# An attention and two expert layers on one core: low halves of w1's block sums on VectorE, and a new order

## The chip, the cores and the metric

The kernel runs on one NeuronCore of one Trainium2 chip. The metric is the device time of one execution in microseconds (us); lower is better. The engines are TensorE (PE; its weight loads are PEld), VectorE (DVE), ScalarE (ACT), GpSimd (POOL) and SyncE (SP), each with a queue of its own that it works through in order. DMAs are issued from SP's and POOL's queues; 16 DMA engines carry them.

## What is computed

Attention first: 2 batches, 8 heads, 768 positions, head size 64. Each query sees the keys less than 16 positions away and 24 block summaries (keys by maximum, values by mean over blocks of 32). Its result, 1536 rows of 512, passes through two layers of experts:

```python
# layer 1: E = 4 experts, D = 512, F = 1024
p = domain_probs / (domain_probs.sum(-1, keepdims=True) + 1e-09)
for e in range(E):
    h = np.maximum(x @ w1[e], 0.0)
    out += p[:, e:e + 1] * (h @ w2[e])
# layer 2: the same with 8 experts; P comes from softmax-like logits
# x @ w_gate and 8 rounds of row and column normalization
```

All inputs and the output are float32.

## The kernel before

**Products.** Rows are taken in two blocks of 768 (b = 0, 1). The hidden size is cut into units of 256 columns: 4 experts x 4 units in layer 1, 8 x 4 in layer 2, 48 units. A step is one unit with one block, so there are 96 steps. In each step a 2x2 block product is made by a scheme of seven products with sums of blocks in place of eight. The seven operands on the side of the weights are the blocks A11, A12, A22 and the sums S1, S2, S3, S4. Each product runs in three parts, because a float32 operand is split into a high half (rounded to the format float32r) and a low half (what is left): high x high, high x low, low x high. `product` (L294 is its matmul) makes the first product, x with w1: seven calls of six matmuls. `add_second` (L593) makes the product with w2: seven operands, two column halves, three matmuls each. One step is 84 matmuls of 128x384. Between them `add_hop` takes the rectified and weighted results (the quads q11 to q22), forms their seven block sums on DVE, and splits each into halves: the high one by ACT (`hi_op`, L453), the low one by DVE (`lo_op`, L443 and L448).

**Weights.** `add_weights(u, kind, start)` (L455) brings the weights of unit u, kind 1 for w1 and 2 for w2. SP loads four blocks into one of three raw buffers (two named `raw`, the third is `xf` once the attention is done with it). The inner function `group` splits n blocks: ACT copies them as the high half (L471), ACT writes their negative into the place of the low half, rounded in the same way (L472), and POOL issues a DMA that adds the raw blocks onto it (L475). What stays is the rest of the rounding. First this is done for the three plain blocks; then three adding DMAs in the raw buffer (L482) turn the raw blocks into sums; then `group` is called for the pair S1, S2 (slots 6 and 7 of `wop`) and the pair S4, S3 (slots 8 and 9). The plain blocks have two sets of slots, by turns; the sums have one, so that a pair can be written only when PE has finished with the last unit's pair.

**The order.** Nothing is issued as the code is read. `op`, `vop` (DVE) and `aop` (ACT) enter each operation into a list with its engine, a name in the table `SPAN`, what it reads and writes, and a due time in units of a step. `run_work` (L367) then plans: it always takes the operation that can start earliest by the prices of `SPAN`, and of several with the same start the one with the earliest due time, and issues it. So the prices and due times alone fix the order in every queue. An entry of `SPAN` is (busy time, time until the result is there). DMAs have four numbers: busy, time until the transfer starts, the length of the transfer on one shared line of DMAs, and the time to landing after that. `add1` to `add3` are the adding DMAs, with lengths of ADD, 2 ADD and 3 ADD.

**Constants.** `ALONG` is the span of due times of the attention, in steps, `XDUE`, `W0DUE` and `FIRST0` the due times of the first operands, weights and products beside it. `NARROW` is the pair of heads from which the attention has five banks of PSUM and not eight. `XPOOL` names the low halves of x that POOL makes. `FIRST` is the order of the seven first products. `HOP`, `GOFF`, `DCOFF`, `LEAD` and `LEAD2` are offsets of the hop, the second products, their second column half, the weights' loads, and the weights' sums. `LATER` and `SOONER` shift the steps around `border`, the last step of layer 1. There `add_turn` makes the next layer's x, and `add_gate` and `add_sinkhorn` its shares.

Of the kernel before, what the change touches and what calls it, by code (L numbers as in the profile page):

```python
# [9 lines left out]
F32 = mybir.dt.float32  # L10
# [8 lines left out]
def local_global_attention_moe_moe(  # L19
# [86 lines left out]
    def wkey(kind, u, a):  # L106
        s = slot(u, a)
        return ("w", kind, s // 3 if s < 6 else 2 + (s - 6) // 2)
# [24 lines left out]
    for b in range(2):  # L133
        for j, name in enumerate(("c22", "c12", "z", "m2", "m1")):
            for c in range(KH):
                i = j * KH + c
# [131 lines left out]
    def pair_of(kind, u, i):  # L268
        r = raw_of(kind, u)
        return ((r[:, 1:3], (1, 2)), (r[:, 0:4:3], (0, 3)))[i]  # L270
# [36 lines left out]
    def relu(S, out, src, th, neg=False):  # L307
# [9 lines left out]

    ADD = 0.72  # L320
    SPAN = {
# [5 lines left out]
        "v1536": (1.3, 1.34), "vmax": (0.57, 0.65), "vsum": (0.57, 0.66), "vrec": (0.12, 0.18),  # L327
        "vks": (0.6, 0.69), "vks2": (0.35, 0.42), "vkw": (0.7, 0.81), "vq": (1.0, 1.1),
        "vvb": (0.22, 0.3), "vmk": (0.82, 0.83), "vid": (1.1, 1.15),
        "a": (0.41, 0.48), "ah": (0.42, 0.52), "a512": (0.53, 0.63), "a768": (0.74, 0.84),  # L330
        "as": (0.2, 0.26), "akw": (0.8, 0.91), "aq": (0.95, 1.04), "aexp": (1.05, 1.12),
        "ax": (0.31, 0.38),
        "p256": (0.75, 0.77), "p384": (1.05, 1.08), "psm": (0.98, 1.02), "pks": (0.8, 0.85),
        "pid": (0.55, 0.6), "p1": (0.2, 0.25), "pmask": (3.0, 3.1), "psel": (0.9, 0.95),
        "add1": (0.87, 1.2, ADD, 1.2), "add2": (0.87, 1.2, 2 * ADD, 1.2),
        "add3": (0.87, 1.2, 3 * ADD, 1.2), "ld": (0.45, 1.0, 0.6, 1.8), "st": (0.45, 0.5, 0.5, 1.2),
        "ldk": (0.45, 1.0, 0.8, 1.2), "ldv": (0.45, 1.0, 1.3, 1.2), "lds": (1.4, 1.6, 1.2, 1.2),
        "ldp": (0.45, 1.0, 0.5, 1.2),
    }
    HOP_WAIT = 0.09  # L340
    work = []
# [94 lines left out]
    def aop(fn, reads, writes, due, span="a", use=None):  # L436
        op("ACT", span, reads, writes, due, fn, use=use)
# [17 lines left out]
    def add_weights(u, kind, start):  # L455
        hi, lo = wop[kind]
        i = turn_of(kind, u)
        R = [("raw", i, j) for j in range(4)]
        for o, x, blocks in loads(kind, u):
            first = XF if (kind, u) == (1, 2) else []  # L460
            op(
                "SP", "ld", [("mark", WAIT0)] if u == 0 else (),
                [R[j] for j in blocks] + first, start,
                lambda o=o, x=x: nc.sync.dma_start(out=o, in_=x),
            )

        def group(s, src, blocks, key, due, span):
            n = len(blocks)
            h, l = hi[:, s:s + n], lo[:, s:s + n]
            rd = [R[j] for j in blocks]  # L470
            aop(lambda: nc.scalar.copy(out=h, in_=src), rd, [key + ("hi",)], due, span)  # L471
            aop(lambda: nc.scalar.mul(l, src, -1.0), rd, [key + ("lo",)], due, span)  # L472
            op(
                "POOL", f"add{n}", rd, [key + ("lo",)], due + 0.05,
                lambda: nc.gpsimd.dma_start(out=l, in_=src, accum_op=ALU.add),  # L475
            )

        group(slot(u, A12), raws[i][:, 0:3], (0, 1, 2), wkey(kind, u, A12), start + 0.2, "a768")
        for o, x, wr, rd in sums_of(kind, u):
            op(  # L480
                "POOL", f"add{len(wr)}", [R[j] for j in (*rd, *wr)], [R[j] for j in wr], start + 0.5,
                lambda o=o, x=x: nc.gpsimd.dma_start(out=o, in_=x, accum_op=ALU.add),  # L482
            )
        group(6, *pair_of(kind, u, 0), wkey(kind, u, S1), start + LEAD2, "a512")
        group(8, *pair_of(kind, u, 1), wkey(kind, u, S4), start + LEAD2 + 0.1, "a512")

    def wk(kind, u, x):
        k = wkey(kind, u, x)
# [506 lines left out]
    def add_loads(i, d):  # L995
        b, hp = pairs[i]
        for j in range(2):
            op(
                "SP", "ldk", (), [("kn", j)] + ([("mark", i)] if j else []), d,
                lambda j=j: nc.sync.dma_start(  # L1000
                    out=kn[:, :, j, :], in_=k[b, 2 * hp + j].rearrange("(c p) d -> p c d", p=P)
                ),
            )
        for j in range(2):
            op(
                "SP", "ldk", (), [("qn", j)], d + 0.01,
                lambda j=j: nc.sync.dma_start(
                    out=qn[:, j],
                    in_=q[b, 2 * hp + j].rearrange("(c p r) d -> p c (r d)", p=P, r=2),
                ),  # L1010
            )
        op(
            "SP", "ldv", (), ["vn"], d + 0.3,
            lambda: nc.sync.dma_start(
                out=vn, in_=v[b, 2 * hp:2 * hp + 2].rearrange("h (p c) d -> p h c d", c=VC)
            ),
        )
        t = vs[i % 2]

        def windows(j):  # L1020
            src = v[b, 2 * hp + j]
            mid = bass.AP(
                src.tensor, src.offset + (QT - WIN) * D, [[D, KW], [QT * D, NQ - 2], [1, D]]
            )
            nc.sync.dma_start(out=t[0:KW, 0, j, :], in_=src[0:KW, :])
            nc.sync.dma_start(out=t[0:KW, 1:NQ - 1, j, :], in_=mid)
            nc.sync.dma_start(out=t[0:KW, NQ - 1, j, :], in_=src[S - KW:S, :])

        for j in range(2):
            op("SP", "lds", (), [("vs", i % 2, j)], d + 0.35, lambda j=j: windows(j))  # L1030

    def add_keys(i, d):
# [50 lines left out]
        def spread():  # L1083
# [4 lines left out]
                )  # L1088

        op(  # L1090
            "POOL" if KSPOOL else "DVE", "pks" if KSPOOL else "vks",
            [("ks", p, 0), ("ks", p, 1)], [("kw", p, 2)], d + 0.03, spread,
        )

# [152 lines left out]
    def add_rows_first(d):  # L1247
# [15 lines left out]
                in1=dsum[:, :, None].to_broadcast([P, NTT, E1]), op=ALU.mult,  # L1263
            )

        vop(shares, ["dp"], ["p1"], d, "v768", True)
        tk = take_of(0)
        n = E1 * NTT
        op(
# [22 lines left out]
            )  # L1292

        aop(halves, ["wg"], ["wghi"], d + 4.0, "as")
        vop(lows, ["wghi", "ident"], ["wghl"], d + 4.0, "vs", True)

    def set_places():

# [18 lines left out]
    L = E1 * NFU - 1  # L1317
    steps = [(u, b, 2 * u + b) for u in range(NU) for b in range(2)]
    border = 2 * L + 1
    FIRST = {0: "1567324", 1: "1562374"}  # L1320
    SECOND = {0: "1256437", 1: "1524637"}
    HOP, GOFF, DCOFF, LEAD, LEAD2 = 1.15, 0.16, 3.9, 1.0, 0.97
    LOPOOL = ()
    ALONG = 8.8
    NARROW = 4
    WAIT0 = 2
    KSPOOL = False
    XDUE = [-5.4, -2.8, -2.0, 0.3]
    W0DUE = -3.0
    FIRST0 = -1.1  # L1330
    XPOOL = [(B22, T3), (N1, B21, T3, N4), (T3, N4), (B22, N4)]
    LATER = {1: -0.4, 2: -0.4, 3: 0.6, 8: -0.4}
    SOONER = {0: 0.4, 2: -0.4, 3: -0.4, 6: 0.2, 7: 0.2}
    TURN = 0.8
    M2ACT = True
    with tc.manual_schedule():
        ps = ctx.enter_context(tc.tile_pool(name="ps", bufs=1, space=PSUM))
        full = [ps.tile([P, 512], F32, name=f"bank{i}") for i in range(8)]
# [33 lines left out]
        op("SP", "ld", ["prow1"], [("pb", 1)], -0.5, lambda: load_row(PB[1], 0, 0, 1))  # L1372
        for j, key in enumerate(("pz", ("bank", 3), ("bank", 4), ("bank", 5), ("bank", 6))):
            op(
                "PE", "one", [("x", 0, 0, B11)] + wk(1, 0, A11), [key], 0.1,
                lambda j=j: nc.tensor.matmul(
                    cut[2 + j], wop[1][0][:, SLOT[A11], 0:P], x_of(0, 0, 0, B11),
                    start=True, stop=True, skip_group_check=True,
                ),
            )  # L1380
# [65 lines left out]
```

## Time and profile before

| | |
|---|---|
| median of 3 runs | 1564.73 us (1563.39 to 1567.13) |
| profiled execution | 1563.7 us, span 1562.0 us |
| PE, PEld busy | 1522.5, 1489.1 us |
| DVE, ACT, POOL busy | 1303.5, 1201.3, 608.7 us |
| DMA | 231.13 MB, mean 148 GB/s |
| granted clock of PE, mean | 0.997 |

Busy time is the union of an engine's instructions within the span; issuing instructions of a queue's sequencer are not counted. The ends of matmuls are modelled, so the idle time of PE is what can be read, not how near it is to its peak. A wait names the instruction or DMA that ended it. Names of tiles are the program's own, without numbers: `w2lo` is the low half of w2's operands, `bank` a bank of PSUM, `hoph` a half of a hop operand, `vn` the tile of v.

### The profile page before, as it was taken

The numbers are of one execution on the slowest core, as the hardware profiler recorded it, in microseconds if no ns is written. First come the engines' busy times: TensorE is split into PE (matmuls) and PEld (weight loads), VectorE is DVE, ScalarE is ACT, GpSimd is POOL, SyncE is SP. The second block draws the span as 40 slices with busy tenths as digits, with TensorE's granted clock in tenths as the row PEclk, the third lists the DMA queues.
The fourth block names the chain that finished last, engine by engine and source line by source line (L and its number), as shares of the span: only waits on it lengthen the run. The fifth ranks groups of instructions, "written<-read, shape, count | busy, mean of one in ns | idle before, by whom it ended". The sixth has DMA issues, their size and how long they took to land.

```text
span 1562.0 us, 26666 instructions
## 1 busy us (share of the span) xinstructions
PE 1522.5 (97%) x9106; PEld 1489.1 (95%) x9106; DVE 1303.5 (83%) x2717; ACT 1201.3 (77%) x2587; POOL 608.7 (39%) x632
## 2 busy tenths in 40 slices
PE   8899999999999999999999999999999999999998
PEld 7799999999999988999999999999999999999997
DVE  7787788788888897899888888888888887888888
ACT  6798688687777779777777778777877877868865
POOL 3553434434343332333343343443434343443430
PEclk9999999999999999999999999999999999999999
DMA  9978888878778874697878778878878887888863
GB/s 213 219 152 148 149 154 149 150 146 153 147 149 149 149 130 94 120 182 133 149 142 156 149 139 161 153 139 155 146 139 159 149 145 150 150 149 150 151 108 95
DMA packets 223865, 231.13 MB, mean 148 GB/s; under 512 B 48736, under 2 KB 169968, under 8 KB 223728
## 3 DMA queue, kind: packets, MB, share of 16 engines
q0 software_dynamic: 107520, 151.03, 60.6%
q1 hardware_dynamic: 116208, 78.39, 17.9%
q8 instruction: 71, 1.16, 0.3%
q14 instruction: 66, 0.54, 0.1%
HBM read 73.97 MB, written 3.22 MB: 49 GB/s over the span
## 4 chain that ended last, share of the span: by engine, by line
PE 72%; DMA 14%; DVE 5%; issue 4%; ACT 3%; POOL 2%; SPq 0%; POOLq 0%; ACTq 0%; DVEq 0%
PE bank L294 34%; PE bank L593 33%; DMA w2lo<-raw 4%; DMA w1lo<-raw 2%; DMA w2lo<-xf 2%; DMA w1lo<-xf 2%; DMA raw<-raw 2%; DVE acc L229 1%; PE bank L1168 1%; DMA vn<-in_v_dram 1%; PE bank L1132 1%; PE bank L1229 1%; ACT hoph L453 1%; PE bank L1214 1%; DVE hoph L448 1%
## 5 line engine op out<-in xcount | busy, mean ns | idle before, releaser
L593 PE MATMUL bank<-hoph,w2hi 128*128 128x384 f32 x2688 | 687.9, 336 | 9.0 <-ACT bank L604 6.1
L593 PEld LDWEIGHTS bank<-hoph,w2hi 128*128 128x128 f32 x2688 | 483.1, 188 | 14.8 <-ACT bank L604 8.3
L593 PE MATMUL bank<-hoph,w2lo 128*128 128x384 f32 x1344 | 451.8, 336 | 8.7 <-DMA w2lo<-raw 6.0
L229 DVE TENSOR_TENSOR acc<-bank,acc 128x384 f32<-128x384 f32 x736 | 392.5, 551 | 7.0 <-PE bank L593 5.0
L294 PE MATMUL bank<-xhi,w1hi 128*128 128x384 f32 x1008 | 339.7, 337 | 1.8 <-ACT xhi L453 1.1
L294 PE MATMUL bank<-xlo,w1hi 128*128 128x384 f32 x1008 | 337.8, 335 | 0.4 <-DVE xlo L443 0.4
L294 PE MATMUL bank<-xhi,w1lo 128*128 128x384 f32 x1008 | 337.6, 335 | 0.2 <-DMA w1lo<-xf 0.2
L482 POOL DMA_DIRECT2D raw<-raw x195 | 194.7, 1000 | 304.3 <-DMA raw<-raw 182.6
L604 ACT COPY bank<-bank 128x384 f32<-128x384 f32 x384 | 181.1, 472 | 153.8 <-PE bank L593 146.8
L453 ACT ACTIVATE hoph<-q 128x384 fp32r<-128x384 f32 x576 | 288.6, 519 | 7.7 <-PE bank L593 4.3
L448 DVE TENSOR_TENSOR hoph<-q,hoph 128x384 fp32r<-128x384 f32 x486 | 259.7, 549 | 27.1 <-ACT hoph L453 26.9
L593 PEld LDWEIGHTS bank<-hoph,w2lo 128*128 128x128 f32 x1344 | 252.2, 188 | 15.2 <-DMA w2lo<-raw 10.6
L294 PEld LDWEIGHTS bank<-xhi,w1hi 128*128 128x128 f32 x1008 | 189.5, 188 | 5.4 <-ACT xhi L453 1.4
L294 PEld LDWEIGHTS bank<-xlo,w1hi 128*128 128x128 f32 x1008 | 189.6, 188 | 0.7 <-DVE xlo L443 0.7
L294 PEld LDWEIGHTS bank<-xhi,w1lo 128*128 128x128 f32 x1008 | 189.5, 188 | 0.5 <-DMA w1lo<-xf 0.5
L475 POOL DMA_DIRECT2D w1lo<-raw x96 | 95.3, 993 | 173.8 <-ACT w1lo L472 136.1
L482 POOL DMA_DIRECT2D xf<-xf x93 | 92.3, 992 | 166.1 <-DMA xf<-xf 101.0
L604 ACT COPY acc<-bank 128x384 f32<-128x384 f32 x220 | 105.0, 479 | 56.3 <-PE bank L593 46.6
L475 POOL DMA_DIRECT2D w2lo<-raw x99 | 108.5, 1098 | 93.4 <-ACT w2lo L472 53.5
L604 ACT COPY bank<-acc 128x384 f32<-128x384 f32 x176 | 85.1, 483 | 55.3 <-DVE acc L229 51.5
L311 DVE SCALAR_TENSOR_TENSOR q<-bank,pb 128x384 f32<-128x384 f32 x180 | 99.5, 553 | 23.2 <-PE bank L294 18.9
L232 DVE TENSOR_TENSOR q<-q,bank 128x384 f32<-128x384 f32 x96 | 53.1, 553 | 71.0 <-PE bank L294 68.1
(180 smaller groups left out, 2168.3 us busy)
## 6 DMA issues: line engine op xcount, KB each, us to landing
raw<-raw POOLq DMA_DIRECT2D x130, 256.0 KB, 3.8
raw<-in_moe_w_dram SPq DMA_DIRECT2D x66, 256.0 KB, 5.0
w2lo<-raw POOLq DMA_DIRECT2D x66, 256.0 KB, 4.1
raw<-in_moe_w_dram SPq DMA_DIRECT2D x128, 128.0 KB, 3.3
w1lo<-raw POOLq DMA_DIRECT2D x64, 256.0 KB, 4.0
xf<-xf POOLq DMA_DIRECT2D x62, 256.0 KB, 3.8
w2lo<-raw POOLq DMA_DIRECT2D x33, 384.0 KB, 5.4
w1lo<-raw POOLq DMA_DIRECT2D x32, 384.0 KB, 5.7
```

The costliest lines, as they stand in the source:

```text
L229: (eng or nc.vector).tensor_tensor(out=out, in0=x, in1=y, op=ALU.add)
L232: (eng or nc.vector).tensor_tensor(out=out, in0=x, in1=y, op=ALU.subtract)
L294: nc.tensor.matmul(pm, l[:, s, cs_], x_of(b, c, r, x), start=first and i == 0, stop=i == n - 1, skip_group_check=True,)
L311: nc.vector.scalar_tensor_tensor(out=out, in0=src, scalar=0.0, in1=PB[S[1]][:, th * HB:(th + 1) * HB], op0=ALU.min if neg else ALU.max, op ...
L448: e.tensor_tensor(out=out, in0=src, in1=hi.bitcast(F32), op=ALU.subtract)
L453: aop(lambda: nc.scalar.mul(to(0), src, -1.0 if neg else 1.0), reads, writes, due, "ah")
L475: lambda: nc.gpsimd.dma_start(out=l, in_=src, accum_op=ALU.add),
L482: lambda o=o, x=x: nc.gpsimd.dma_start(out=o, in_=x, accum_op=ALU.add),
L593: nc.tensor.matmul(cut[bank], l[:, s, cols], hop_of(t, r), start=start and i == 0, stop=i == 2, skip_group_check=True,)
L604: aop(lambda: nc.scalar.copy(out=out, in_=src), [kin], [kout], due)
L1132: nc.tensor.matmul(pv[KW:KX, 0:P], sel[:, c, :], vn[:, :, c, :], start=c == 0, stop=c == VC - 1,)
L1168: nc.tensor.matmul(pw[:, tt * KX:(tt + 1) * KX], bd[p][:, g * GT + tt].rearrange("x j q -> x (j q)"), kw[p][(g * GT + tt) // KT][:, (g * G ...
```

## The change

`group` has a new argument. Where it is set, the low half is one subtraction on DVE, raw minus high half, and neither the negating cast on ACT nor the adding DMA on POOL is issued. `LODVE` sets it for both pairs of w1's sums in all 48 units; w2's groups and w1's plain blocks are as before. Prices of DMAs in `SPAN`, some names in it (a price of its own for an operation that shared one), and the constants of the order are set anew. The order `FIRST` of block 1 changes. No other operation is added or removed; with `XPOOL`, which engine makes some low halves of x changes.

```diff
-    ADD = 0.72
+    ADD = 0.85
...
-        "vks": (0.6, 0.69), "vks2": (0.35, 0.42), "vkw": (0.7, 0.81), "vq": (1.0, 1.1),
-        "vvb": (0.22, 0.3), "vmk": (0.82, 0.83), "vid": (1.1, 1.15),
+        "vks": (0.6, 0.69), "vksw": (0.600001, 0.69), "vks2": (0.35, 0.42), "vkw": (0.7, 0.81), "vq": (1.0, 1.1),
+        "vvb": (0.22, 0.3), "vsh": (0.870001, 0.97), "vlow": (0.150001, 0.2), "dum": (0.110002, 0.3), "vmk": (0.82, 0.83), "vid": (1.1, 1.15),
...
-        "add1": (0.87, 1.2, ADD, 1.2), "add2": (0.87, 1.2, 2 * ADD, 1.2),
-        "add3": (0.87, 1.2, 3 * ADD, 1.2), "ld": (0.45, 1.0, 0.6, 1.8), "st": (0.45, 0.5, 0.5, 1.2),
-        "ldk": (0.45, 1.0, 0.8, 1.2), "ldv": (0.45, 1.0, 1.3, 1.2), "lds": (1.4, 1.6, 1.2, 1.2),
-        "ldp": (0.45, 1.0, 0.5, 1.2),
+        "add1": (0.95, 1.3, ADD, 1.2), "add2": (0.950001, 1.3, 2 * ADD, 1.2),
+        "add3": (0.950002, 1.3, 3 * ADD, 1.2), "ld": (0.45, 1.0, 0.65, 1.3),
+        "st": (0.450001, 0.5, 0.5, 1.2), "ldk": (0.450002, 1.0, 1.2, 1.2),
+        "ldq": (0.450003, 1.0, 0.6, 1.2), "ldv": (0.450004, 1.0, 1.0, 1.2),
+        "lds": (1.4, 1.6, 1.8, 1.2), "ldp": (0.450005, 1.0, 0.6, 1.2),
...
-        def group(s, src, blocks, key, due, span):
+        def group(s, src, blocks, key, due, span, by_dve=False):
...
+            if by_dve:
+                vop(
+                    lambda: vsub(l, src, h.bitcast(F32)), rd + [key + ("hi",)],
+                    [key + ("lo",)], due + 0.05, "v512",
+                )
+                return
...
-        group(6, *pair_of(kind, u, 0), wkey(kind, u, S1), start + LEAD2, "a512")
-        group(8, *pair_of(kind, u, 1), wkey(kind, u, S4), start + LEAD2 + 0.1, "a512")
+        for i, s in enumerate((S1, S4)):
+            group(
+                SLOT[s], *pair_of(kind, u, i), wkey(kind, u, s), start + LEAD2 + i / 10, "a512",
+                (kind, s) in LODVE,
+            )
...
-                "SP", "ldk", (), [("qn", j)], d + 0.01,
+                "SP", "ldq", (), [("qn", j)], d + 0.01,
...
-            "POOL" if KSPOOL else "DVE", "pks" if KSPOOL else "vks",
+            "POOL" if KSPOOL else "DVE", "pks" if KSPOOL else "vksw",
...
-        vop(shares, ["dp"], ["p1"], d, "v768", True)
+        vop(shares, ["dp"], ["p1"], d, "vsh", True)
...
-        vop(lows, ["wghi", "ident"], ["wghl"], d + 4.0, "vs", True)
+        vop(lows, ["wghi", "ident"], ["wghl"], d + 4.0, "vlow", True)
...
-    FIRST = {0: "1567324", 1: "1562374"}
+    FIRST = {0: "1567324", 1: "1567342"}
     SECOND = {0: "1256437", 1: "1524637"}
-    HOP, GOFF, DCOFF, LEAD, LEAD2 = 1.15, 0.16, 3.9, 1.0, 0.97
+    HOP, GOFF, DCOFF, LEAD, LEAD2 = 1.19, 0.15, 5.8, 1.0, 0.94
     LOPOOL = ()
-    ALONG = 8.8
-    NARROW = 4
+    ALONG = 5.4
+    NARROW = 6
     WAIT0 = 2
     KSPOOL = False
-    XDUE = [-5.4, -2.8, -2.0, 0.3]
-    W0DUE = -3.0
-    FIRST0 = -1.1
-    XPOOL = [(B22, T3), (N1, B21, T3, N4), (T3, N4), (B22, N4)]
-    LATER = {1: -0.4, 2: -0.4, 3: 0.6, 8: -0.4}
-    SOONER = {0: 0.4, 2: -0.4, 3: -0.4, 6: 0.2, 7: 0.2}
+    XDUE = [-3.1, -2.5, -1.5, 0.6]
+    W0DUE = -1.6
+    FIRST0 = 0.1
+    XPOOL = [(B11, B21, B22, T3), (N1, T3, N4), (B21, N4), (B11, N4)]
+    LATER = {-2: -0.2, 1: -0.4, 2: 0.8, 3: 1.0, 6: -0.2, 8: -0.2}
+    SOONER = {0: 0.6, 1: -0.2, 2: 0.2, 3: 0.4, 6: 0.4, 7: 0.2}
     TURN = 0.8
     M2ACT = True
+    LODVE = ((1, S1), (1, S4),)
...
-                "PE", "one", [("x", 0, 0, B11)] + wk(1, 0, A11), [key], 0.1,
+                "PE", "dum", [("x", 0, 0, B11)] + wk(1, 0, A11), [key], 0.1,
```

## Rows read from the trace of the kernel before

**Rows 1.** The page's part on busy time, whole span.

```profile
PE 1522.5 (97%) x9106; PEld 1489.1 (95%) x9106; DVE 1303.5 (83%) x2717; ACT 1201.3 (77%) x2587; POOL 608.7 (39%) x632
```

**Rows 2.** Windows: length, busy us (count) of PE, PEld, DVE, ACT, POOL, clock, DMA, GB/s.

```profile
0.00:110.00 110.00, 96.80 (x963) 85.36 (x964) 87.20 (x202) 85.05 (x231) 50.79 (x69) 0.98 0.95 201
110.00:560.00 450.00, 445.54 (x2544) 441.03 (x2544) 368.70 (x744) 350.87 (x744) 182.23 (x184) 1.00 0.80 147
560.00:740.00 180.00, 172.50 (x970) 162.18 (x970) 160.34 (x386) 142.75 (x308) 62.24 (x63) 0.99 0.71 133
740.00:1540.00 800.00, 792.90 (x4541) 787.90 (x4541) 670.88 (x1355) 613.55 (x1290) 313.46 (x317) 1.00 0.79 144
1540.00:1562.00 22.00, 14.77 (x94) 12.60 (x92) 16.36 (x33) 9.11 (x19) 0.00 (x0) 0.96 0.38 144
```

**Rows 3.** Waits of PE, whole span: total us, times, longest us.

```profile
PE bank L593 <- ACT bank L604: 6.1, 7, 2.5
PE bank L593 <- DMA w2lo<-raw: 6.0, 13, 1.2
PE bank L1132 <- DMA vn<-in_v_dram: 6.0, 3, 2.8
...
PE bank L593 <- DMA w2lo<-xf: 2.4, 4, 0.8
PE bank L1214 <- POOL s L1205: 1.8, 2, 1.3
```

**Rows 4.** Instruction groups by form: count, busy us, mean ns, idle before.

```profile
L475 POOL DMA_DIRECT2D w1lo<-raw x96 | 95.3, 993 | 173.8 <-ACT w1lo L472 136.1 <-PE bank L294 24.6 <-PE bank L593 7.6
...
L472 ACT ACTIVATE w1lo<-raw 128x512 fp32r<-128x512 f32 x64 | 40.5, 634 | 0.0
...
L471 ACT CAST w1hi<-raw 128x512 fp32r<-128x512 f32 x64 | 39.4, 616 | 11.5 <-PE bank L294 7.5 <-DMA raw<-raw 3.9
...
L472 ACT ACTIVATE w1lo<-xf 128x512 fp32r<-128x512 f32 x32 | 20.3, 635 | 0.0
...
L1071 DVE TENSOR_REDUCE acc<-bank 128x16 f32<-128x512 f32 x8 | 5.5, 690 | 3.6 <-ACT kw L1064 1.7 <-ACT acc L1240 0.6 <-ACT kwa L1064 0.6
...
L1071 DVE TENSOR_REDUCE acc<-bank 128x8 f32<-128x256 f32 x8 | 3.3, 407 | 0.0
```

**Rows 5.** Timeline of DVE in a steady step: start, duration, instruction.

```profile
917.07 0.55 DVE L229 TENSOR_TENSOR acc<-bank,acc 128x384 f32<-128x384 f32 x1
917.54 0.55 DVE L448 TENSOR_TENSOR hoph<-q,hoph 128x384 fp32r<-128x384 f32 x1
```

**Rows 6.** DMA queue of POOL, and issues by line (KB, median us to landing).

```profile
q0 software_dynamic: 107520, 151.03, 60.6%
...
w2lo<-raw POOLq DMA_DIRECT2D x66, 256.0 KB, 4.1
...
w1lo<-raw POOLq DMA_DIRECT2D x64, 256.0 KB, 4.0
```

**Rows 7.** Timelines of PE, ACT and POOL around one refill of the w2 sums.

```profile
813.39 0.33 PE L593 MATMUL bank<-hoph,w2lo 128*128 128x384 f32 x1
...
814.49 0.61 ACT L471 CAST w2hi<-raw 128x512 fp32r<-128x512 f32 x1
...
815.93 0.90 POOL L475 DMA_DIRECT2D w2lo<-raw  x1 [1.08 <-PE bank L294]
...
820.51 0.44 PE L593 MATMUL bank<-hoph,w2lo 128*128 128x384 f32 x1 [0.16 <-DMA w2lo<-raw]
```

**Rows 8.** Windows of 5 us in the turn between the layers, columns as in Rows 2.

```profile
585.00:590.00 5.00, 5.00 (x31) 4.84 (x30) 5.00 (x13) 4.69 (x12) 0.00 (x0) 1.00 0.31 45
```

**Rows 9.** Timelines of POOL and DVE in the attention.

```profile
81.86 0.98 POOL L1205 TENSOR_TENSOR s<-s,sm 128x480 f32<-128x480 f32 x1 [1.83 <-DVE sm L1200]
...
82.28 0.97 DVE L448 TENSOR_TENSOR xlo<-acc,xhi 128x384 fp32r<-128x384 f32 x1
...
84.84 0.55 DVE L448 TENSOR_TENSOR xlo<-acc,xhi 128x384 fp32r<-128x384 f32 x1
```

## The prediction

> **What bounds the kernel now.** I read the page's busy times first: TensorE (PE) is busy 97% of a span of 1562.0 us, VectorE (DVE) 83%, ScalarE (ACT) 77%, GpSimd (POOL) 39% [rows 1]. An engine at 97% is the bound, so a change that gives PE no less work can only win back PE's idle time. This change leaves every matmul as it is. The windows by stage say how much idle time there is [rows 2]: attention, 110 - 96.8 = 13.2 us; first layer, 450 - 445.5 = 4.5; the turn between the layers, 180 - 172.5 = 7.5; second layer, 800 - 792.9 = 7.1; end, 7.2. Together 39.5 us, 2.5% of the span. That is the whole purse, and part of it (the first loads, the last store) no plan can have.
>
> Who ended those idle times is in PE's waits [rows 3]: the adding DMAs of w2's low halves, 6.0 + 2.4 = 8.4 us in 17 waits; ACT's bank copies, 6.1; v's load in the attention, 6.0 in 3 waits; a normalization on POOL, 1.8. The reader should see what is missing: w1's low halves, the ones that the change touches, are not among the large waits. The removed DMAs are slow, but PE did not wait for them. So the edit itself buys nothing directly. It can pay through what it frees, and through the new order.
>
> **The change part by part.** *Removed on ACT and POOL.* 64 + 32 = 96 negating casts of 128x512 at about 0.634 us, 60.8 us of ACT, and 96 issues of adding DMAs at 0.993 us, 95 us of POOL [rows 4]. The DMA queue of POOL moves 151.03 MB [rows 6]; 96 x 256 KB is 25.2 MB of it, a sixth, or about 10 points of its 60.6% of DMA time. None of this was on PE's path. What it frees is room for neighbours. ACT's late copies hold PE for 6.1 us; ACT loses 5% of its load. I take -1.0 us, bounds -6.1 and 0.
>
> *Added on DVE.* 96 subtractions of 128x512. No such row exists. Reductions over 512 and 256 elements take 690 and 407 ns [rows 4], so 283/256 = 1.1 ns an element; a 384-wide subtraction shows 0.55 us, and the next one starts 0.47 us after it [rows 5]. The new one then shows about 0.55 + 0.14 = 0.69 us and holds the queue about 0.61 us: 58.6 us in all. In the two steady stretches DVE is idle 450 - 368.7 + 800 - 670.9 = 210 us [rows 2], which covers it on average. In the turn it is idle only 180 - 160.3 = 19.7 us, and in stretches not at all [rows 8]. A unit lasts two steps; 84 matmuls a step and 4541 in 800 us make 14.8 us a step, so 180 us hold 6 units, 12 subtractions, 7.3 us. Nine windows of 5 us, from 560 to 605, read as the one shown: 45 us are fully booked, 3 subtractions. I take +1.0 us, half of these three, since the due times around the turn also move; bounds 0 and +7.3. If DVE's cover elsewhere were gone, each uncovered subtraction would cost its 0.61 us.
>
> The subtraction adds a wait: it stands in DVE's queue behind ACT's high-half copy, which itself sat idle 11.5 us before its groups, for PE and for raw sums that had not landed [rows 4]. Everything behind it on DVE (gates, hop differences, accumulations) waits too, and PE waits for those. That is the price tag of the slower rival below.
>
> *The order planned anew.* This is where I look for the gain. One refill of w2's first pair of sums [rows 7]: the last product that reads the old pair starts at 813.39, ACT copies at 814.49, POOL issues the add at 815.93, and PE, which had got there earlier, starts the low-half product at 820.51. The planner of before prices a two-block add at 1.2 + 2 x 0.72 + 1.2 = 3.84 us from issue to landing; the new one at 1.3 + 2 x 0.85 + 1.2 = 4.20. The trace has 4.1 as the median [rows 6]. So the old planner put the product about a third of a microsecond too early, and the mean wait is 8.4 / 17 = 0.49 us. With 0.36 us more in the price, 17 x 0.36 = 6.1 us of waits should be filled with other products. I take -6.0; bounds -8.4 (all) and +2 (the spread of landings finds new victims). The new DCOFF works against this. In units of a step, the distance by due times from the last use of the old pair to the first use of the new one was 1 + 2/10.9 - 7.9/10.9 = 0.46 (6.8 us) and is now 1 + 2/12.8 - 9.8/12.8 = 0.39 (5.8 us). But due times only break ties among work that the planner thinks ready, and by its longer price the product is ready later.
>
> *The attention.* The due times of its 24 groups now spread over 5.4 steps, not 8.8, the banks are narrowed later, and loads of k, q, v and of v's windows have prices of their own. The instructions and DMAs are the same; the order on SP's and POOL's queues moves. v's load accounts for 6.0 us of PE's idle time and the normalization behind other POOL work for 1.8 [rows 3]. Better DMA prices should save one of the three waits for v, 2.0 us. Bounds: -7.8 (all) and +5.6 (two more of the longest, 2.8). I take -2.0. POOL's low halves of x go from 10 listed to 11, no sum.
>
> A row here bears on DVE's added work: a 128x384 subtraction that started at 82.28, while POOL worked on a tile in SBUF from 81.86 to 82.84, took 0.97 us; one at 84.84 with POOL's tensor work done took 0.55 [rows 9]. [...] By it the new subtractions of the first two units, four at most, would each lose up to 0.42 us, 1.7 us in all, and the forecast would be 1558.4; by DVE's idle share of the attention they lose nothing that PE sees. In the steady stretches POOL only issues DMAs.
>
> *The sum.* -1.0 + 1.0 - 6.0 - 2.0 = -8.0 us. The profiled execution took 1563.7 us (1562.0 of span and 1.7 around it), so 1555.7. The median of the runs is 1.0 above the profiled one: **1556.7 us**.
>
> **Rivals.**
> *A, the forecast* (0.54): own range 1551 to 1562. For it: the old price is below the traced landing, and the waits of w2's low halves recur all through both layers.
> *B, nothing that counts is touched* (0.16): the refill of w2 keeps its casts, issues and DMAs, PE finds it just as late, and the attention's order comes out even. Left are -1.0 and +1.0: 1564.7 us. For it: w2's path has the same instructions, and DCOFF shortens the distance. Against it: the price is longer.
> *C, the queue of DVE becomes the bound* (0.17): the subtraction sits behind a late high-half copy and holds gates and hop differences. If one in four of the 96 is uncovered, 24 x 0.61 = 14.6 us, and the time is 1571.3. From 13 uncovered ones on, the 8 us of gain are gone; from 18 on the kernel is slower by more than a measurement can tell. For it: the turn shows DVE booked to the last tenth. Against it: 210 us of idle DVE in the steady stretches.
> *D, the order gains wherever it can* (0.13): all 8.4 us of w2's waits, 3 of ACT's, 6 of the attention's, nothing lost in the turn: 1564.7 - 17.4 = 1547.3. Against it: landings vary, so some waits always stay.
>
> **How the numbers follow.** Two runs of this kernel can be told apart from about 0.2%, 3.1 us: same is 1561.6 to 1567.9. Faster takes A and D, 0.67; same B, 0.16; slower C, 0.17. The range reaches to D's time, a little below, and most of the way to C's, which leaves out about 0.2: 1546 to 1569; A's own range stands above.
>
> **What would show it.** Right: 96 DVE subtractions of about 0.69 us at the group's line, ACT's and POOL's groups for w1 down to the 48 of three blocks, PE's waits for w2's low halves near 2 to 3 us, PE's idle time down by about 8 us with DVE near 87%. A wait of PE for w1's high or low half, or for gates and hop halves of DVE in the steady stretches, would show C. Waits for w2's low halves still near 8 us would show B. The forecast is wrong outright if the attention's window, up to the first products without attention between them, grows by more than 5 us, because nothing later could pay that back.

## The result, and the profile after

The changed kernel takes 1546.53 us, the median of 4 runs (1541.35 to 1547.48), against 1564.72 before: ratio 0.9875 with a 95% interval of 0.985 to 0.990, so 18.2 us less. I had forecast 1556.7, 8 us less. The range holds the measured time, and the direction was right, but the gain is more than twice the forecast, nearest to rival D (1547.3). On another chip, beside later experiments, it took 1544.19 us, ratio 0.9852 (0.9832 to 0.9871).

The profiled execution took 1545.96 us with a span of 1544.2, 17.8 less than before's 1562.0. First the page's busy times and the windows by stage, which answer to [rows 1, 2]:

```profile
PE 1513.4 (98%) x9106; PEld 1490.9 (97%) x9106; DVE 1353.8 (88%) x2812; ACT 1155.2 (75%) x2491; POOL 508.8 (33%) x537
```

```profile
0.00:110.00 110.00, 98.19 (x995) 88.38 (x996) 93.58 (x211) 88.60 (x236) 51.74 (x70) 1.00 0.96 199
110.00:560.00 450.00, 446.56 (x2570) 445.50 (x2569) 394.35 (x796) 342.68 (x726) 151.31 (x155) 1.00 0.71 134
560.00:740.00 180.00, 173.23 (x957) 164.56 (x958) 160.60 (x382) 134.84 (x288) 49.69 (x51) 0.96 0.58 112
740.00:1540.00 800.00, 795.44 (x4587) 792.50 (x4586) 705.28 (x1426) 589.10 (x1242) 256.05 (x261) 1.00 0.67 129
```

DVE has 50 us more, ACT 46 less, POOL 100 less. By the end of every stage PE has got through more matmuls in all. Who still ends its idle times answers to [rows 3]:

```profile
PE bank L1052 <- DMA kn<-in_k_dram: 5.9, 2, 4.4
PE bank L294 <- ACT xhi L454: 3.7, 1, 3.7
PE bank L294 <- DVE q L311: 2.9, 2, 1.5
...
PE bank L603 <- ACT bank L614: 1.8, 2, 0.9
...
PE bank L1142 <- DMA vn<-in_v_dram: 0.5, 1, 0.5
```

The adding DMAs of w2's low halves are gone from the list, and so is most of v's load. Left are the first loads (k), and VectorE's and ScalarE's chain in the turn between the layers. The groups of the changed lines answer to [rows 4, 6]:

```profile
L232 DVE TENSOR_TENSOR w1lo<-raw,w1hi 128x512 fp32r<-128x512 f32 x64 | 43.7, 683 | 0.7 <-ACT w1hi L472 0.7
...
L482 POOL DMA_DIRECT2D w1lo<-raw x32 | 27.7, 867 | 83.2 <-ACT w1lo L479 63.9 <-PE bank L603 14.4 <-ACT hoph L454 3.6
...
L232 DVE TENSOR_TENSOR w1lo<-xf,w1hi 128x512 fp32r<-128x512 f32 x32 | 21.9, 684 | 0.2 <-DMA raw<-in_moe_w_dram 0.2
```

```profile
q0 software_dynamic: 87552, 125.86, 51.0%
...
w2lo<-raw POOLq DMA_DIRECT2D x66, 256.0 KB, 4.1
```

The subtraction takes 0.683 us, where I had estimated 0.69; VectorE stood idle ahead of all 96 for 0.7 and 0.2 us in total. The landing of w2's add is 4.1 us, the same median as before.

To see where the 17.8 us went I cut both traces at the starts of the same matmuls, counted among those of 128x384 with w1 or w2 as weights: the first of step 4, of step 31, of step 40 and of step 95. The times are those starts, subtracted; a step has 84.

| stretch | before | after | difference | forecast |
|---|---|---|---|---|
| attention and 4 steps | 158.5 | 151.4 | -7.1 | -2.0 |
| steps 4 to 31 | 400.8 | 393.8 | -7.1 | the two steady stretches together: -7.0 |
| steps 31 to 40, the turn | 158.8 | 165.2 | +6.3 | +1.0 |
| steps 40 to 95 | 814.2 | 802.1 | -12.1 | (above) |
| last step and end | 29.7 | 31.8 | +2.1 | 0 |

The last row goes with the new constants for the most part: in e3, e9 and e10 below, which have the old ones, it is 0.0. The steady steps are the main thing: -19.2 us. The same window of both kernels shows it best, before and then after:

```profile
740.00:1500.00 760.00, 752.90 (x4311) 747.91 (x4311) 635.02 (x1283) 586.66 (x1232) 304.23 (x308) 1.00 0.81 149
```

```profile
740.00:1500.00 760.00, 760.00 (x4379) 760.00 (x4379) 670.08 (x1356) 567.02 (x1195) 253.94 (x259) 1.00 0.69 131
```

After, PE and its weight loads are busy in all 760.00 us, with 4379 matmuls against 4311. That is 0.1736 us a matmul, 14.58 a step: with the same matmuls nothing is left to gain there by order. Before, 68 matmuls fewer at 0.1736 are 11.8 us lost, though the same row shows only 760 - 752.9 = 7.1 us of idle PE.

### The profile page after: what moved, and what is told of

Same layout as the page of the kernel before. It is cut to its first block, busy times and chain, and to the rows that moved or that the text cites. A ratio compares the mean times of both kernels' runs of the same rounds, so it can differ in the third digit from the quotient of the medians.

```text
span 1544.2 us, 26702 instructions
## 1 busy us (share of the span) xinstructions
PE 1513.4 (98%) x9106; PEld 1490.9 (97%) x9106; DVE 1353.8 (88%) x2812; ACT 1155.2 (75%) x2491; POOL 508.8 (33%) x537
## 4 chain that ended last, share of the span: by engine, by line
PE 90%; DVE 6%; ACT 2%; DMA 1%; issue 1%; SPq 0%; DVEq 0%; ACTq 0%
PE bank L294 44%; PE bank L603 43%; DVE acc L229 2%; PE bank L1178 1%; PE bank L1239 1%; DVE hoph L449 1%; PE bank L1142 1%; PE bank L1224 0%; DVE acc L235 0%; DVE q L311 0%; DVE acc L232 0%; DMA acc<-in_v_dram 0%; PE bank L781 0%; ACT hoph L454 0%; DMA kn<-in_k_dram 0%
## 5 line engine op out<-in xcount | busy, mean ns | idle before, releaser
L489 POOL DMA_DIRECT2D raw<-raw x195 | 199.6, 1035 | 360.1 <-DMA raw<-raw 113.2
L454 ACT ACTIVATE hoph<-q 128x384 fp32r<-128x384 f32 x576 | 299.8, 525 | 17.1 <-DVE q L311 7.2
L449 DVE TENSOR_TENSOR hoph<-q,hoph 128x384 fp32r<-128x384 f32 x486 | 264.0, 553 | 9.4 <-ACT hoph L454 9.2
L482 POOL DMA_DIRECT2D w2lo<-raw x99 | 100.6, 1020 | 211.0 <-ACT w2lo L479 170.9
L489 POOL DMA_DIRECT2D xf<-xf x93 | 95.4, 1026 | 173.2 <-DMA xf<-xf 52.1
L514 ACT ACTIVATE q<-bank 128x384 f32<-128x384 f32 x192 | 94.2, 492 | 20.6 <-PE bank L294 20.0
L311 DVE SCALAR_TENSOR_TENSOR q<-q,pb 128x384 f32<-128x384 f32 x180 | 99.0, 551 | 1.5
```

The source lines that it names most:

```text
L311: nc.vector.scalar_tensor_tensor(out=out, in0=src, scalar=0.0, in1=PB[S[1]][:, th * HB:(th + 1) * HB], op0=ALU.min if neg else ALU.max, op ...
L449: e.tensor_tensor(out=out, in0=src, in1=hi.bitcast(F32), op=ALU.subtract)
L454: aop(lambda: nc.scalar.mul(to(0), src, -1.0 if neg else 1.0), reads, writes, due, "ah")
L514: aop(lambda: nc.scalar.mul(out, src, by), [kin], [kout], due)
```

## The experiments

What had to be told apart: is it the edit (less work on ACT, POOL and the DMA engines), the prices (the planner knows how long an add takes), or the constants (due times and the rest)? And which of them acts where?

**Edit, prices, constants, one by one.** Each kernel takes the edit (S), the new prices (P) and the new constants (C) or leaves them as before. The edits, as lines that differ:

```diff
# e1: before, with group(..., by_dve) and
+    LODVE = ((1, S1), (1, S4),)
# e2: after, with
-    LODVE = ((1, S1), (1, S4),)
+    LODVE = ()
# e3: before, with the new SPAN and ADD = 0.85
# e7: after, with the old SPAN and ADD = 0.72
# e9: after, with FIRST, HOP ... LEAD2, ALONG, NARROW, XDUE, W0DUE, FIRST0,
#     XPOOL, LATER and SOONER of before
# e10: e1, with only
-    ADD = 0.72
+    ADD = 0.85
-        "add1": (0.87, 1.2, ADD, 1.2), ...
+        "add1": (0.95, 1.3, ADD, 1.2), ...      # add2, add3 alike
```

Edit alone (e1), expected: 

> The VectorE subtractions for both pairs of w1, planned with the prices and constants of the kernel before. Theory 'order' (the gain comes from new prices and constants): 1564 us, within 4 us of the kernel before, and PE's waits for w2's low halves stay near 8 us. Theory 'relief' (96 casts and 96 adding DMAs less free ACT, POOL and the DMA engines, and that is what ends PE's waits): at least half of the 18 us, 1556 or below, with the w2 waits under 3 us. Rival 'queue of DVE': above 1568.

Order alone (e2), expected: 

> The new prices and constants without the subtractions: w1's sums by cast and adding DMA as before. Theory 'order': 1546 to 1552 us, with PE's waits for w2's low halves under 3 us. Theory 'relief': 1558 us or above, the waits for low halves come back, and ACT is at 77% again.

Prices alone (e3), expected: 

> Only the prices of DMAs in the table are new; constants and instructions are those of the kernel before. Theory 'order' in its narrow form, as I predicted (the two-block add is priced 0.36 us longer, and that fills the waits): about 1557 us, w2 waits near 2 us. If prices alone don't pay and only the constants set beside them do: 1562 to 1572 us.

Old prices (e7), expected: 

> The subtractions and the new constants, planned with the old prices of DMAs. Theory 'order' by prices: the w2 waits are back near 6 to 8 us, 1554 us or above. Theory 'relief': prices don't matter, 1545 to 1550 us.

Old constants (e9), expected: 

> The subtractions, planned with the new prices of DMAs but all constants of the order as before. Theory 'prices' (the edit pays once the planner knows how long an add takes, the constants add little): 1546 to 1552 us, PE's waits for w2's low halves under 2 us. Theory 'constants' (the edit pays only with an order set for it): 1558 us or above, not better than the prices alone, which gave 1559. If the edit with new prices still has w2 waits over 8 us, as the edit with old prices had (25), the price of an add is not what went wrong there.

Price of adds only (e10), expected: 

> The subtractions with all constants and all other prices of before; only the adding DMAs are priced anew (ADD 0.85 instead of 0.72, start 1.3 instead of 1.2 us). With old prices this edit took 1598 us, with all new prices 1551.5. If the price of an add is what the planner had wrong: 1550 to 1558 us and PE's waits for w2's low halves under 3 us. If the loads' prices matter as much: 1565 to 1590 us, with those waits at 8 us or more.

Measured; each ratio is to runs of the kernel before on the same chip. The last three columns are differences to before in the stretches above, one profile each, "steady" being steps 4 to 31 and 40 to 95:

| kernel | S | P | C | us | ratio to before (95%) | attention | steady | turn |
|---|---|---|---|---|---|---|---|---|
| e1 | x | | | 1598.06 | 1.0218 (1.0188 to 1.0248) | +3.5 | +22.2 | +7.3 |
| e3 | | x | | 1558.98 | 0.9964 (0.9950 to 0.9979) | +1.7 | -14.7 | +8.1 |
| e2 | | x | x | 1569.96 | 1.0036 (1.0024 to 1.0048) | +3.9 | -7.8 | +9.4 |
| e7 | x | | x | 1567.46 | 1.0009 (0.9994 to 1.0025) | +8.4 | -11.6 | +8.9 |
| e10 | x | adds | | 1553.06 | 0.9920 (0.9906 to 0.9934) | -1.9 | -18.8 | +6.6 |
| e9 | x | x | | 1551.53 | 0.9892 (0.9859 to 0.9926) | -0.7 | -19.0 | +8.2 |
| after | x | x | x | 1546.53 | 0.9875 (0.9850 to 0.9900) | -7.1 | -19.2 | +6.3 |

The three do not add up. Take one away from the changed kernel, and it loses 23 us (e2, without the edit), 21 us (e7, without the prices) or 5 us (e9, without the constants, in overlapping intervals). The edit is worth 23 us beside new prices and constants, some 7 us beside the new prices (e3 to e9), and by itself it costs 34 us. The constants alone, the one combination left, were not run.

The waits of PE in e1, the edit by itself:

```profile
PE bank L602 <- DMA w2lo<-raw: 17.5, 11, 3.0
PE bank L602 <- DMA w2lo<-xf: 7.9, 8, 2.2
```

They are 25.4 us, three times the 8.4 of before, and the window of 760 us has 4228 matmuls, 83 fewer than before's 4311:

```profile
740.00:1500.00 760.00, 743.42 (x4228) 737.98 (x4227) 655.32 (x1311) 553.19 (x1156) 244.89 (x250) 0.99 0.67 128
```

Both of my theories missed e1: "order" said 1564, "relief" 1556 or below, and the rival "queue of DVE" had the side right but not the cause. DVE was busy 655 of 760 us, and what PE waited for was the DMAs that the edit does not touch. One price puts it right. In e10 the edit is the same and only adds are priced anew; a two-block add has 4.20 us from issue to landing, not 3.84:

```profile
740.00:1500.00 760.00, 760.00 (x4380) 759.97 (x4379) 673.07 (x1357) 568.43 (x1200) 255.29 (x261) 1.00 0.70 132
```

No wait for a low half of the weights is left among PE's waits, of which these are some:

```profile
PE bank L1141 <- DMA vn<-in_v_dram: 6.2, 4, 3.9
PE bank L602 <- ACT bank L613: 5.0, 4, 2.6
...
PE bank L602 <- DVE hoph L448: 1.4, 2, 1.0
```

1598 became 1553 by the price of one kind of DMA in the planner's table; the rest of the prices (e9) changed nothing that these runs can tell. But the price is not the only thing that ends the loss. e7 has the edit and the old price of adds, and with the new constants its waits for w2's low halves are 3.3 us, not the 6 to 8 that I expected, and its steady steps are 11.6 us shorter than before's:

```profile
PE bank L602 <- DMA w2lo<-raw: 2.7, 3, 1.2
...
PE bank L602 <- DMA w2lo<-xf: 0.6, 1, 0.6
```

Prices without the edit (e3) gain 14.7 us in the steady steps, with 0.3 us of waits for w2's low halves:

```profile
PE bank L603 <- ACT bank L614: 5.6, 7, 2.6
...
PE bank L1142 <- DMA vn<-in_v_dram: 1.9, 3, 1.0
...
PE bank L603 <- DMA w2lo<-xf: 0.3, 1, 0.3
```

```profile
740.00:1500.00 760.00, 759.61 (x4375) 759.21 (x4374) 643.76 (x1302) 588.10 (x1252) 310.57 (x314) 1.00 0.81 151
```

From there the edit adds the last 4.5 us of the steady steps: -14.7 to -19.0 in e9. Constants add nothing in the steady steps once edit and prices are there (e9 and after end alike), and without the edit they spoil them (e2). e2 thus fell on the side of "relief", though w2's waits are only 1.9 us there; why the new constants need the edit is not shown. A likely reason for e1 is that in the plan all adds share one line of DMAs: two fewer on it let the plan put w2's adds, and the products behind them, earlier, and the too short price is no longer covered by waiting in the line. That is argued from the planner's code. The traces add that w2's two-block adds land later in e1 than in e10, where they land as priced; the medians of e1 and then of e10:

```profile
w2lo<-raw POOLq DMA_DIRECT2D x66, 256.0 KB, 4.4
```

```profile
w2lo<-raw POOLq DMA_DIRECT2D x66, 256.0 KB, 4.2
```

Those that ended PE's 19 waits in e1 took 4.6 to 5.7 us, against the plan's 3.84. The add behind the longest wait, 3.0 us, landed after 4.82 us, so its 0.98 us beyond the plan are not all of that wait; the rest stays open. What is shown is that the adds' price alone is enough to remove the loss.

**The attention.** The gain of 7.1 us there needs all three: without the constants it is 0.7 (e9), and without the edit (e2) or the prices (e7) the stretch is 3.9 and 8.4 us longer than before. Three kernels split the constants:

```diff
# e4: after, with the six constants of the attention as before
# e14: after, with only
+    NARROW = 4
+    XPOOL = [(B22, T3), (N1, B21, T3, N4), (T3, N4), (B22, N4)]
# e17: after, with only
+    ALONG = 8.8
+    XDUE = [-5.4, -2.8, -2.0, 0.3]
+    W0DUE = -3.0
+    FIRST0 = -1.1
```

Expected of e4: 

> The changed kernel with the attention's constants (ALONG, NARROW, XDUE, W0DUE, FIRST0, XPOOL) of before. If these constants make the 7 us that the first four steps gained: 1552 to 1556 us, with all of the loss before 160 us. If it is the freed ACT, POOL and DMA time and the prices: 1545 to 1549 us.

Expected of e14: 

> The changed kernel with NARROW and XPOOL of before (the banks of the attention, and which low halves of x GpSimd makes); the due times stay new. All six constants of before lost 7.6 us in the first four steps. If the banks and GpSimd's share make it: 1550 to 1554 us. If the due times make it: 1545 to 1548 us.

Expected of e17: 

> The complement: the due times of the attention (ALONG, XDUE, W0DUE, FIRST0) of before, NARROW and XPOOL new. If the due times make the gain of the first four steps: 1550 to 1555 us, and PE waits for v or for POOL's normalization again. If not: 1545 to 1548 us.

Measured: e4 1551.69 us (0.9900, 0.9867 to 0.9933), e14 1547.79 (0.9870, 0.9852 to 0.9887), e17 1554.44 (0.9920, 0.9903 to 0.9937). Attention and four steps take 159.0, 156.7 and 160.8 us, against 151.4, and 153.0 in the repeat of the changed kernel beside e14 and e17. So the due times are worth 7.8 to 9.4 us there (160.8 less 153.0 or 151.4); the banks and GpSimd's share 3.7 to 5.3 in the traces, with overlapping intervals in the times. These parts do not add up either: with all six old (e4) the stretch is shorter than with the due times alone. With the old due times PE waits longer for POOL's normalization; e17 up to 110 us, and then the repeat of the changed kernel:

```profile
PE bank L1224 <- POOL s L1215: 6.5, 5, 2.4
...
PE bank L1142 <- DMA vn<-in_v_dram: 1.6, 3, 0.8
```

```profile
PE bank L1224 <- POOL s L1215: 1.8, 1, 1.8
```

**More subtractions.** Would both pairs of w2's sums gain too?

```diff
-    LODVE = ((1, S1), (1, S4),)
+    LODVE = ((1, S1), (1, S4), (2, S1), (2, S4))
```

Expected: 

> The changed kernel with both pairs of w2's sums by subtraction too: 96 more on VectorE (0.68 us each, some 58 us of its queue), 96 adding DMAs and casts less. Theory 'PE is free of waits already': the steady steps can't gain, 1543 to 1550 us. Theory 'queue of DVE' (my rival C, at 92% busy instead of 88%): 1556 us or above, with PE's waits on VectorE and on ACT's hop halves in the steady steps.

Measured: 1550.4 us, ratio 0.9892 (0.9853 to 0.9931), about 4 us slower than the changed kernel, within overlapping intervals. The steady steps don't change at all:

```profile
740.00:1500.00 760.00, 760.00 (x4379) 759.96 (x4379) 700.99 (x1410) 537.99 (x1147) 199.30 (x208) 1.00 0.58 114
```

DVE is busy 701 of 760 us there, 92%, and PE still 760.00. The 96 subtractions fit there. The turn of e8 takes 169.4 us instead of 165.2 (161.9 in the repeat of the changed kernel).

**The turn.** It is longer than before in every kernel with new prices or the edit, in e3 by 8.1 us without one subtraction. In the changed kernel PE stands at 557 for a high half from ACT, and then this follows (timeline of PE: start, duration, instruction):

```profile
556.95 0.34 PE L294 MATMUL bank<-xlo,w1hi 128*128 128x384 f32 x1
557.12 0.34 PE L294 MATMUL bank<-xhi,w1lo 128*128 128x384 f32 x1
561.17 0.69 PE L294 MATMUL bank<-xhi,w1hi 128*128 128x384 f32 x1 [3.71 <-ACT xhi L454]
...
564.11 0.52 PE L294 MATMUL bank<-xhi,w1hi 128*128 128x384 f32 x1
564.43 0.52 PE L294 MATMUL bank<-xlo,w1hi 128*128 128x384 f32 x1
```

Matmuls start 0.17 us apart before the wait and 0.32 us apart after it, until 570. The granted clock is down in the same stretch (windows of 5 us, the third number from the end):

```profile
560.00:565.00 5.00, 3.66 (x10) 2.56 (x11) 5.00 (x12) 2.75 (x6) 2.99 (x3) 0.52 0.69 107
565.00:570.00 5.00, 5.00 (x18) 4.54 (x18) 4.53 (x10) 1.27 (x4) 1.20 (x1) 0.50 0.50 73
```

It was 0.52 and 0.50 at the end of PE's wait of 3.7 us and after it, against 1.00 in the three windows from 545 to 560. By these distances I estimate that the 9 us of slow matmuls, from 561 to 570, cost 9 x (1 - 0.174/0.32) = 4.1 us at most, if nothing else would have held PE meanwhile. Two kernels fill the wait with matmuls that nobody needs, to see whether the clock then stays up:

```diff
# e11: in product(), ahead of the first matmul of that product
+        for _ in range(FILL.get((n_, a), 0)):       # 22 at step 32, A12
+            nc.tensor.matmul(pm, hi[:, s, 0:P], x_of(b, 0, 0, x), start=True, stop=True, ...)
# e12 and e19: in add_gate(), ahead of the first matmul of the gate
+                    for _ in range(FILL.get((b, len(terms), lo_), 0)):    # 22, once
+                        y = x_of(b, 0, 0, B11)
+                        nc.tensor.matmul(cut[7], y[:, 0:P], y, start=True, stop=True, ...)
```

e11 overwrites a partial sum that the product should add to, so it leaves out a part of the result; e12 writes where the gate overwrites.

Expected of e11: 

> The changed kernel with 22 more matmuls of 128x384 put before the first product of the turn that waits (result thrown away), where PE idled 3.7 us at 557 and then took 0.32 us a matmul, not 0.17, until 570. Theory 'clock' (the idle time lowers the granted clock, and the 9 us at half speed after it are a cost of their own, 4.6 us): the granted clock stays 1.00 there and the time is 1540 to 1543 us. Theory 'wait only' (PE would wait for VectorE's chain of the turn anyway, whatever its clock): 1545 to 1548 us; if the added matmuls delay the product, 1548 to 1551.

Expected of e12: 

> The changed kernel with 22 more matmuls of 128x384 ahead of the first gate matmul of the turn, into the bank that the gate then overwrites, so that nothing of the result changes. Theory 'clock': as with the fillers before, the granted clock stays 1.00 from 555 to 575 and the time is 1541 to 1544 us. Theory 'wait only': 1545 to 1548 us.

Expected of the repeat on one chip, e18, the changed kernel: 

> The changed kernel once more, beside the next ones on one chip: 1544 to 1548 us, the granted clock of 560 to 575 near 0.5 to 0.6.

And e19, the fillers: 

> The changed kernel with the 22 fillers ahead of the gate once more: if the clock's part is real, 2 to 4.6 us under the changed kernel on the same chip.

Measured: e11 1543.06 us (ratio 0.9840, 0.9808 to 0.9872), e12 1543.45 (0.9859, 0.9847 to 0.9872), and side by side e18 1544.19 (0.9852, 0.9832 to 0.9871) and e19 1544.07 (0.9846, 0.9829 to 0.9863). In e19 the clock is 1.00 in this stretch; the same windows of e18 and then of e19:

```profile
560.00:565.00 5.00, 2.06 (x5) 1.21 (x6) 5.00 (x12) 2.56 (x5) 2.08 (x2) 0.63 0.68 109
565.00:570.00 5.00, 5.00 (x22) 4.29 (x21) 5.00 (x11) 2.35 (x5) 2.11 (x2) 0.69 0.51 74
```

```profile
560.00:565.00 5.00, 4.59 (x25) 3.48 (x24) 5.00 (x11) 2.86 (x6) 2.09 (x2) 1.00 0.67 106
565.00:570.00 5.00, 4.37 (x23) 3.28 (x23) 5.00 (x12) 3.11 (x8) 2.11 (x2) 1.00 0.45 65
```

So the clock was low with this wait in both profiles of the changed kernel (0.52 and 0.50, 0.63 and 0.69 in e18), and 1.00 with fillers in it: in e11 and e12 from 540 to 580, in e19 from 550 to 575. That the fillers pay is not shown: on one chip the two medians lie 0.1 us apart. In e18 the low stretch was shorter than in the first profile, and its turn took 161.9 us, against 161.0 in e12 and 162.6 in e19. In e19 the clock fell once later: 0.73 and 0.93 from 700 to 710, where e18 has 1.00. Repeats of the changed kernel spread over 6 us, and those at 1545.9 and above show a mean clock of 0.994 or 0.995, those at 1544.3 and below 0.997 or 0.998; the repeats of e11, e12 and e19 all show 0.998 or 0.999, at 1541.18 to 1545.40. The fillers may take away the slow end. These few runs leave that open.

**VectorE's load in the turn.** e15 gives some of it to GpSimd, e16 does that and fills the wait:

```diff
# e15: in add_turn()
-                lo_op("DVE", to, src, [key, k + (0,)], [k], d, neg)
+                eng = "POOL" if i in (N2, N4) and not neg else "DVE"
+                lo_op(eng, to, src, [key, k + (0,)], [k], d, neg)
# e16: e12 and e15 together
```

Expected of e15: 

> The changed kernel with the low halves of N2 and N4 of the turn (8 of 28) made by GpSimd, not VectorE: some 8 x 0.47 = 3.8 us less on VectorE in the stretch where it is booked to the last tenth. Theory 'the turn is bound by VectorE': the turn shortens by 2 to 6 us, 1541 to 1545 us. Theory 'the chain of sums, not the load': 1545 to 1549 us; GpSimd takes 1.0 to 1.3 us for one, so if PE waits for those it is above 1549.

Expected of e16: 

> The fillers ahead of the gate and the low halves of N2 and N4 of the turn on GpSimd, together. If the two act on different costs (clock and VectorE's load): 1537 to 1541 us. If they take away the same idle time: as the better of the two, 1541 to 1545 us.

Measured: e15 1554.5 us (0.9933, 0.9921 to 0.9945), e16 1550.9 (0.9913, 0.9899 to 0.9926). Both lose; the turn of e15 takes 170.2 us, and from 560 to 570 the granted clock was 0.76 in e15 and, with the fillers, 0.83 in e16. PE still waits for the same high half, and more for the copies behind it:

```profile
PE bank L294 <- ACT xhi L454: 3.7, 1, 3.7
...
PE bank L603 <- ACT acc L614: 2.7, 1, 2.7
```

Less load on VectorE did not shorten the turn, so my first theory for e15 is out. The second gave 1545 to 1549 us, and more if PE waits for GpSimd's low halves; such a wait is not in PE's list. The trace shows another cost. Three subtractions of VectorE that lay beside GpSimd's took 1.15, 1.26 and 1.35 us, where 0.55 is usual. In e16 VectorE has 16 instructions in 9.45 busy us from 560 to 570, in e12 22 in 10.00. Here are two of the three in e15, and then GpSimd's two of that time:

```profile
569.82 1.26 DVE L449 TENSOR_TENSOR hoph<-q,hoph 128x384 fp32r<-128x384 f32 x1
571.01 1.35 DVE L449 TENSOR_TENSOR hoph<-t,hoph 128x384 fp32r<-128x384 f32 x1
```

```profile
569.51 2.44 POOL L449 TENSOR_TENSOR xlo<-acc,xhi 128x384 fp32r<-128x384 f32 x2 [1.99 <-ACT xhi L454]
```

The three lost 2.1 us, of the 3.8 that I had hoped to save, and GpSimd's eight took 10.6 us in all (14 halves named `xlo` and `x11xb` from `acc`, 16.6 us, less the 6 that took 6.0 us in the changed kernel). Whether that made the turn longer, or the length of the chain of sums and halves did, these runs do not separate.

## Why the prediction was right in its mechanism and wrong in size

**What bounds, and the purse.** PE is the bound: right. "Together 39.5 us ... That is the whole purse" was where it failed first: not in the total, which was not used up, but in the share of the steady stretches. I took it from PE's idle time. There that is 11.6 us, but the matmuls' starts show 19.2 us lost, because a modelled matmul end (336 ns of duration at 0.17 us from start to start) hides the first 0.16 us of every wait. The number was in my own text: I worked out 14.8 us a step and did not set it beside 84 x 0.1736 = 14.58. 0.22 us times 82 steps is 18 us. PEld's busy column in [rows 2] says it too: 450 - 441.0 + 800 - 787.9 = 21 us.

**The order planned anew, -6.0: right in its cause, mis-sized.** The step "17 x 0.36 = 6.1 us of waits should be filled" names the price of an add as too short, and the runs agree: new prices alone (e3) leave 0.3 us of w2's waits, and beside the edit that one price is worth 45 us (e1, e10). But it sized the gain by 17 listed waits, with all 8.4 us of them as its bound. By starts, waits for w2's low halves cost 11.2 us in the steady steps before, ACT's copies 3.3, and the rest is spread over small gaps. The new prices alone end 14.7 us of these 19.2, where the term had -6.0, and the edit beside them ends the rest. So this is the term that failed, by its size. That DCOFF would work against it did not show in the steady steps: e9 and the changed kernel, 3.9 and 5.8, end alike.

**Removed on ACT and POOL, -1.0.** "So the edit itself buys nothing directly" holds for the edit alone, which costs 34 us. Beside the new prices it buys 4.5 us of the steady steps, within my bounds. Beside new prices and constants it buys 23 us (e2), some 11 each in the attention and the steady steps, far beyond my bound of -6.1: I had added terms that need one another. One row I misread: the 96 issues at 993 ns are 64 of pairs and 32 of three blocks, not the 96 that went. The total was near all the same, 100 us of POOL.

**Added on DVE, +1.0.** Instruction and total were right (0.683 us, 65.6 in all, DVE at 88%). In the turn the changed kernel's plan puts a pair at 544 and 549 and the next at 596 and 600. The one at 549 stands in a stretch that VectorE works through without a gap until PE's wait at 557 ends; what is next there starts 0.60 us later, my price for an uncovered one:

```profile
549.13 0.68 DVE L232 TENSOR_TENSOR w1lo<-raw,w1hi 128x512 fp32r<-128x512 f32 x1
549.73 0.55 DVE L311 SCALAR_TENSOR_TENSOR q<-bank,pb 128x384 f32<-128x384 f32 x1
```

But the turn lost 6.3 us in the first profile and 3.0 in the repeat, and e3 lost 8.1 without any subtraction. The longer wait for the chain and the lowered clock are in it (3.7 us, and 0.52 and 0.50 from 560 to 570, in the first profile); how they share it is open. I had not priced the clock, though [rows 2] showed 0.99 for the turn before.

**The attention, -2.0.** Measured -7.1, -5.5 in the repeat. v's waits went from 6.0 to 0.5 us, and the normalization on POOL from 1.8 to nothing listed, but in the repeat they are 1.6 and 1.8; I had put one of v's three waits. My lower bound, -7.8, held. "Better DMA prices should save one" was too simple: with the prices alone (e3) v's waits fell to 1.9 us, and the stretch still grew by 1.7. The due times (e17) gain only beside the edit and the prices.

**The subtractions beside GpSimd.** From the one row of 0.97 us against 0.55 I had named up to 1.7 us, outside the sum, for the four subtractions of the first two units. They took 0.68, 0.68, 0.69 and 0.69 us, as the mean of all does. The timelines (start, duration, instruction) of VectorE and then of POOL, of the changed kernel, show where the first two lay:

```profile
88.17 0.68 DVE L232 TENSOR_TENSOR w1lo<-raw,w1hi 128x512 fp32r<-128x512 f32 x1
...
89.34 0.68 DVE L232 TENSOR_TENSOR w1lo<-raw,w1hi 128x512 fp32r<-128x512 f32 x1
```

```profile
86.60 1.01 POOL L449 TENSOR_TENSOR xlo<-acc,xhi 128x384 fp32r<-128x384 f32 x1 [4.98 <-ACT xhi L454]
...
90.73 0.98 POOL L1215 TENSOR_TENSOR s<-s,sm 128x480 f32<-128x480 f32 x1 [2.32 <-DVE sm L1210]
```

They lie between two tensor instructions of POOL, from 87.61 to 90.73. The other two start at 116.96 and 117.86, and POOL's last tensor instruction of that stretch starts at 106.25 and takes 1.02 us; from then to 125 it only issues DMAs. So these four do not test what I had named: none lay beside tensor work of POOL. In e15 VectorE's work did, and three subtractions took 1.15 to 1.35 us against 0.55, as told above.

**Rivals.** B is out: w2's waits are gone. C did not happen: VectorE waited under 1 us in all ahead of the subtractions, and e8 shows room for 96 more in the steady steps. D had the time, and two of its three reasons (w2's waits, the attention) with the first twice as large; it did not have the longer turn. That its time, 1547.3, is so near is luck: larger gains and losses that D did not have made it up.

## What to carry to other kernels

Read the lost time of an engine whose instructions overlap, as PE's do in these traces (0.34 us long, 0.17 from start to start), from start to start: the count of instructions times the distance of two unhindered starts, against the window. The idle column left out the first 0.16 us of each wait. In a kernel whose order is planned by a price table, an edit and the prices are one change: with an add priced 0.36 us too short this edit cost 34 us; the edit and that one price together gained 12; and without the edit the new prices and constants gained nothing (e2). So measure the prices again in a trace before judging an edit by itself, and ask of every removal what it may let the plan move closer to a late transfer.

## What the runs showed that I had not expected

After 3.7 us of idle PE the granted clock was 0.52 and 0.50 in the windows from 560 to 570, and 22 matmuls in the wait held it at 1.00 there (e19), without a difference in time that these runs can tell. GpSimd took 8 of 28 low halves of the turn off VectorE, which was busy in all of the 20 us from 545 to 565 in the changed kernel, and the kernel became some 8 us slower (e15); three subtractions of VectorE beside GpSimd's took 1.15, 1.26 and 1.35 us, where 0.55 is usual.
